# A written TensorE order, 96-row transposes and a shorter feed-forward lag in a fused windowed-attention and feed-forward kernel

## The chip, the cores and the metric

The kernel runs on one core of a Trainium2 chip. The metric is the device time of one execution in microseconds (us). The engines are TensorE (PE; its weight loads are PEld), VectorE (DVE), ScalarE (ACT), GpSimd (POOL) and SyncE (SP), which issues most transfers.

## What is computed

Eight batches with eight heads each hold 512 local and 32 global tokens of head dimension 64. A local token attends to the 32 global tokens and to local tokens at most 32 places away; a global token attends to all 544. The outputs of the heads, side by side, are 4608 rows of 512, and go through a feed-forward network with a squared ReLU:

```python
s_g = scale * q_g @ k_all.T;  out_g = softmax(s_g) @ v_all
s_ll = where(abs(i - j) <= 32, scale * q_l @ k_l.T, -1e9)
out_l = softmax(concat([scale * q_l @ k_g.T, s_ll])) @ v_all
x = concat([out_g, out_l]) as 4608 x 512
out = (s * relu(x @ w_in)**2 + b) @ w_out        # 512 -> 2048 -> 512, float32
```

## The kernel before

Most matmul operands are split in two parts of a shorter float32 format (`F32R`): a rounded high part and the remainder. A product of two split operands is then a sum of several matmuls. ACT casts the high part, and DVE or POOL subtracts.

The work is a loop over steps `j`. A step carries one head through a pipeline. There are 128 heads of 256 queries: eight heads of one half of the sequence and then eight of the other make a batch of 16 steps, and eight heads of a half make one tile of 256 tokens. The first 16 heads (`NF`) go in pairs through an unsplit float32 path while the feed-forward weights are loaded and split (`weight_piece`). From head 16 on, a step issues these TensorE groups, which the text calls by a letter:

- **S** and **G** (`scores`, lines 351 and 357): four matmuls of 192 or 224 columns for the local scores of head `j`, and one of 256 or 288 columns with a 64-column weight for the global tokens' scores. DVE masks and finds the maximum (212), ACT takes the exponential (218), DVE scales (227). The global scores are copied by ACT (361) and added by DVE (362) into `sg`.
- **T** (`p_transposes`, line 306): four float32 transposes of the probabilities of head `j - 1`, 128 by 128 each, split by ACT (367) and DVE (368).
- **P** (`pv_products`, line 378): four matmuls of 128, 192 or 256 columns of head `j - 2`, summed by ACT (389) and DVE (390, 392) into the tile of tokens `x`, which has one buffer.
- **F** (`ffn_in`, line 500): 24 matmuls of 256 columns for one eighth of a tile, feed-forward step `m = j - LAG`, then ACT (506, 514) and DVE (507, 515) for ReLU, square and split.
- **A** (`ffn_out`, line 532): 12 matmuls of 512 columns of feed-forward step `m - 1`, in two accumulators of six each.

Eight feed-forward steps make a tile. After the eighth, `x_split` (472 and 473) makes the split tokens of the next tile `xs`, which has one buffer, in two halves of a cast and a subtraction. Twice in a batch the global tokens of four heads have their softmax (`g_softmax`, at the steps `G_AT`), five transposes (`g_transposes`, three steps later), loads and splits of their values (`g_load`) and products of ten matmuls each, **O** (`g_pv`, line 452). Their outputs go to DRAM, and the last tile, number 16, reads them back (`xg_split`).

PSUM has eight banks: one each for S, G (also used by O), T, P and the two accumulators of A, and two for F. All engines' instruction orders are made by the planner of the tile framework. It simulates the engines, takes what is ready, and prefers what stands earlier in the program; within TensorE too it is free to mix the groups of several steps. The order is then fixed in the program, and each engine runs it in sequence.

The steps end as follows in the loop, and `LAG` is 12:

```python
ffn_in(m)                     # then x_split or xg_split when m % 8 == 7
transposes_and_pv(j - 1, j - 2)
vsp(j - 1)
for fn in extra.pop(j, []): fn()
ffn_out(m - 1)
```

Of the kernel before, what the change touches and what calls it, by code (L numbers as in the profile page):

```python
# [10 lines left out]
F32 = mybir.dt.float32  # L11
F32R = mybir.dt.float32r
# [7 lines left out]
B, H, SL, SG, D = 8, 8, 512, 32, 64  # L20
DM, DF = 512, 2048
P = 128
# [8 lines left out]
NC = 416  # L31
# [12 lines left out]

NF = 16
AHEAD = 0
LAG = 12
WARM_FIRST = 28

SPOTS = (["a","b","c","c","xs"]+["c","c","a","b"]*1+["a","b","c","c"]*12)[:32]  # L50
PIECES = [2, 2, 2, 2, 2, 2, 2, 2, 2, 2, 3, 3, 3, 3]
ACT_DMA = 2
X_ACT = lambda i: i >= 4
G_AT = (13, 18)
G_TR = 3
G_LD = (0, 2)
G_PV = (1, 3)
# [4 lines left out]
def f32(ap):  # L62
    return ap.bitcast(F32)
# [3 lines left out]
def window_attention_then_ffn(ctx: ExitStack, tc: tile.TileContext, qd, qp, qg, kw, vw, vg, w_in, w_out, sv, bv, out):  # L67
# [219 lines left out]
    def chunks(j):  # L287
        b, hf, h = slot(j)
        o = 0
        for blk in range(2):  # L290
            for c in range(2):
                c0, q0, n = CHUNKS[hf, blk][c]
                yield blk, c, c0, q0, n, slice(o, o + n)
                o += n
# [4 lines left out]
    def p_transposes(j):  # L299
        sm = st_.pop(("p", j))  # L300
        p_t = ps.tile([P, 512], F32, tag="t", name=f"ps_t{j}")
        first = 64 if slot(j)[1] == 0 else 0
        st_["pst", j] = p_t[:, first:first + NC]
        for blk, c, c0, q0, n, o in chunks(j):
            at = first + o.start - q0
            nc.tensor.transpose(out=p_t[:, at:at + P], in_=sm[:, c0:c0 + P], identity=ident)  # L306
            if c == 1:
                yield

    def transposes32(i):  # L310
        pt = st_["ptp", i] = sb.tile([P, 2, NC], F32, tag="pt", name=f"ptp{i}")
# [32 lines left out]
    def scores(j):  # L344
        b, hf, h = slot(j)
        ks, qs = st_.pop(("ks", j)), st_.pop(("qs", j))
        p_s = ps.tile([P, 512], F32, tag="s", name=f"ps_s{j}")
        for blk in range(2):
            cols = COLS[hf, blk]
            for a in range(2):  # L350
                nc.tensor.matmul(  # L351
                    p_s[:, cols], lhsT=qs[:, a, blk * P:(blk + 1) * P], rhs=ks[:, cols], start=(a == 0), stop=(a == 1),
                )
        p_g = ps.tile([P, 512], F32, tag="g", name=f"ps_g{j}")
        qgh = st_["qgs", b][:, h]
        ng = 256 + 32 * hf
        nc.tensor.matmul(p_g[0:64, 0:ng], lhsT=qgh, rhs=own(ks, hf), start=True, stop=True)
        softmax([j], [p_s])

        tg = sb.tile([P, 288], F32, tag="tg", name=f"tg{j}", bufs=1)  # L360
        nc.scalar.copy(out=tg[0:32, 0:ng], in_=p_g[32:64, 0:ng])
        nc.vector.tensor_add(out=sg_rows(j, 32)[:, hf * 256:hf * 256 + ng], in0=p_g[0:32, 0:ng], in1=tg[0:32, 0:ng])  # L362
# [11 lines left out]
    def pv_products(j):  # L374
        pt, vs = st_.pop(("pt", j)), st_.pop(("vs", j))
        p_o = st_["pso", j] = ps.tile([P, 2, 2, P], F32, tag="o", name=f"ps_o{j}")
        for blk, c, c0, q0, n, o in sorted(chunks(j), key=lambda x: (x[0], -x[1])):
            nc.tensor.matmul(  # L378
                p_o[:, blk, :, q0:q0 + n], lhsT=vs[:, 2 * blk + c], rhs=pt[:, :, o], start=(c == 1), stop=(c == 0),
            )  # L380
            if c == 0:
                yield

    def pv_sum(j):
        b, hf, h = slot(j)
# [11 lines left out]
    def transposes_and_pv(jt, jp):  # L397
        t = p_transposes(jt) if NF <= jt < NS else iter(())
        p = pv_products(jp) if NF <= jp < NS else iter(())
        for _ in range(2):  # L400
            next(p, None)
            next(t, None)
        list(p), list(t)
        if NF <= jp < NS:
            pv_sum(jp)
        if NF <= jt < NS:
            p_split(jt)
# [10 lines left out]
        nc.vector.reciprocal(gs, gs)  # L418
        nc.vector.tensor_scalar_mul(v, v, gs)

    def g_transposes(b, g, c0, c1):
        sg = st_["sg", b, g]
        if c0 == 0:
            st_["pg", b, g] = sb.tile([P, 5, 4, 2, SG], F32R, tag="pg", name=f"pg{b}_{g}", bufs=1)
        pg = st_["pg", b, g]
        if True:
            p_t = ps.tile([P, 4, P], F32, tag="t", name=f"ps_tg{b}_{g}_{c0}")
            for c in range(c0, c1):
                s0 = min(c * P, SGW - P)
                nc.tensor.transpose(out=p_t[:, c - c0, :], in_=sg[:, s0:s0 + P], identity=ident)  # L430
            v = p_t[:, 0:c1 - c0].rearrange("p c (h q) -> p (c h) q", h=4)
            ph, pl = (pg[:, c0:c1, :, i, :].rearrange("p c h q -> p (c h) q") for i in range(2))
            nc.scalar.copy(out=ph, in_=v)
            nc.vector.tensor_sub(out=pl, in0=v, in1=f32(ph))


    def g_load(b, h):
        rv = sb.tile([P, 10 * D], F32, tag="rvg", name=f"rvg{b}_{h}", bufs=1)
# [37 lines left out]
    def xg_split(t):  # L476
        xs = sb.tile([P, 2, 4, HALF], F32R, tag="xs", name=f"xs{t}", bufs=1)
        for i in range(2):
            xr = sb.tile([P, DM], F32, tag="r", name=f"xgr{i}", bufs=2)
            nc.sync.dma_start(xr, xg_d[i * P:(i + 1) * P, :])  # L480
            p_t = ps.tile([P, 4, P], F32, tag="t", name=f"ps_xg{i}")
            for c in range(4):
                nc.tensor.transpose(out=p_t[:, c, :], in_=xr[:, c * P:(c + 1) * P], identity=ident)
            q = slice(i * P, (i + 1) * P)
            nc.scalar.copy(out=xs[:, 0, :, q], in_=p_t)
            nc.vector.tensor_sub(out=xs[:, 1, :, q], in0=p_t, in1=f32(xs[:, 0, :, q]))
        xs_[t] = xs
# [31 lines left out]

    oacc = {}  # L520

    def ffn_out(m):
        t, pr = m // 8, m % 8
        g = gs_.pop(m)
        if pr == 0:
            oacc[t] = [ps.tile([P, DM], F32, tag=f"acc{i}", name=f"acc{t}_{i}") for i in range(2)]
        for i in range(2):
            n = 0
            for k in range(2):
                f = 2 * pr + k  # L530
                for a, e in ((0, 0), (0, 1), (1, 0)):
                    nc.tensor.matmul(  # L532
                        oacc[t][i], lhsT=g[:, a, k, i * P:(i + 1) * P], rhs=wo[:, e, f, :],
                        start=(pr == 0 and n == 0), stop=(pr == 7 and n == 5),
                    )
                    n += 1
        if pr == 7:
            for i in range(2):
                o = sb.tile([P, DM], F32, tag="r", name=f"o{t}_{i}", bufs=2)
                nc.scalar.copy(out=o, in_=oacc[t][i])  # L540
                if t < 16:
                    b, hf = t // 2, t % 2
                    r0 = b * (SL + SG) + SG + hf * HALF + i * P
                    nc.sync.dma_start(out[r0:r0 + P, :], o)
                else:
                    rows = out.rearrange("(b r) d -> b r d", r=SL + SG)[4 * i:4 * i + 4, 0:SG, :]
                    nc.sync.dma_start(rows, o)
# [2 lines left out]
    nc.sync.dma_start(b_t, bv.partition_broadcast(P))  # L550

    NM = NT * 8
    extra, early, late = defaultdict(list), {}, {}
    for b in range(B):
        for g in range(2):
            s0 = 16 * b + G_AT[g]
            extra[s0].append(lambda b=b, g=g: g_softmax(b, g))
            early[s0 + G_TR] = lambda b=b, g=g: g_transposes(b, g, 0, 4)
            late[s0 + G_TR] = lambda b=b, g=g: g_transposes(b, g, 4, 5)
            for i in range(2):  # L560
                h = 4 * g + 2 * i
                extra[s0 + G_TR + G_LD[i]].append(lambda b=b, h=h: g_load(b, h))
                extra[s0 + G_TR + G_PV[i]].append(lambda b=b, h=h: g_pv(b, h))
# [18 lines left out]
    qg_load(0)  # L582
    ld(0)
    ld(2)
    for j in range(NM + LAG + 2):
        sp(j + 1)
        if j + 4 < NF:
            ld(j + 4)
        if j + 2 >= NF:
            ld(j + 2)  # L590
        vl(j)
        for _ in range(PIECES[j] if j < len(PIECES) else 0):
            weight_piece(piece)
            piece += 1
        if j < NS:
            b1 = j // 16 + 1
            if j % 16 == 14 and b1 < B:
                qg_load(b1)
            sc(j)
            if j % 16 == 15 and NF <= j + 1 < NS:  # L600
                qg_split(b1)
        if j in early:
            early.pop(j)()
        m = j - LAG
        if 0 <= m < NM:
            ffn_in(m)
            if m % 8 == 7:
                t = m // 8 + 1
                if t < 16:
                    x_split(t)  # L610
                elif t == 16:
                    xg_split(16)
        tr(j - 1)
        transposes_and_pv(j - 1, j - 2)
        vsp(j - 1)
        for fn in extra.pop(j, []):
            fn()
        pvs(j - 2)
        if j == 0:
            vl32(0)  # L620
        vl32(j + 2)
        if j == 9:
            x_split(0)
        if 0 <= m - 1 < NM:
            ffn_out(m - 1)
        if j in late:
            late.pop(j)()
    assert piece == 32 and not extra


# [73 lines left out]
```

## Time and profile before

| | |
|---|---|
| time, median of 3 runs | 1049.52 us (1049.19 to 1052.2) |
| time of the profiled execution | 1050.66 us |
| its span, first to last instruction | 1048.0 us |
| mean granted TensorE clock | 0.986 |
| PE busy | 1008.9 us (96%), 7060 matmuls |
| PEld busy | 908.8 us (87%) |
| DVE busy | 816.4 us (78%) |
| ACT busy | 710.1 us (68%) |
| POOL busy | 311.8 us (30%) |

Busy time is the time in which an engine has at least one instruction in work. Matmuls overlap: the recorded duration of one is longer than the distance to the next. The profile is of one execution; the times are of others of the same program.

### The profile page before, as it was taken

How to read it: one execution, taken by the hardware profiler on the slowest of the kernel's cores; microseconds unless marked ns; L12 is line 12 of the kernel's file. 1: busy time of each engine (PE TensorE's matmuls, PEld its weight loads, DVE VectorE, ACT ScalarE, POOL GpSimd, SP SyncE). 2: the span in 40 equal slices, each digit the busy share in tenths (PEclk: the TensorE clock that was granted, in tenths of full speed). 3: DMA queues.
4: the chain of work that ended last, by engine and by line, in shares of the span. 5: the costliest groups of instructions: out<-in, count | busy, mean ns of one | idle time of the engine just before them, and what ended most of it. 6: DMA issues, size and time to landing. Idle time of an engine off the chain costs nothing.

```text
span 1048.0 us, 20280 instructions
## 1 busy us (share of the span) xinstructions
PE 1008.9 (96%) x7060; PEld 908.8 (87%) x7060; DVE 816.4 (78%) x2096; ACT 710.1 (68%) x1816; POOL 311.8 (30%) x365
## 2 busy tenths in 40 slices
PE   6689999999999999999999999999999999999996
PEld 3378999989999899989998899988998899999895
DVE  6999878887798878888798778888699778863321
ACT  6997867777587667777587667777687667743221
POOL 0000634333343324333343324333343324211000
PEclk8789999999999999999999999999999999999998
DMA  8764322312132222312132122312132122101000
GB/s 297 255 218 142 95 65 72 95 47 91 48 114 57 62 66 76 96 47 91 47 111 60 54 74 76 96 48 90 48 109 62 49 80 67 55 2 48 22 21 20
DMA packets 62254, 85.73 MB, mean 82 GB/s; under 512 B 7368, under 2 KB 49352, under 8 KB 62152
## 3 DMA queue, kind: packets, MB, share of 16 engines
q1 hardware_dynamic: 61864, 83.39, 25.8%
q8 instruction: 55, 0.90, 0.4%
q10 hardware_dynamic: 288, 1.05, 0.3%
q14 instruction: 47, 0.39, 0.1%
HBM read 74.97 MB, written 9.44 MB: 81 GB/s over the span
## 4 chain that ended last, share of the span: by engine, by line
PE 62%; DVE 22%; ACT 10%; issue 3%; DMA 2%; DVEq 0%; ACTq 0%; SPq 0%
PE acc L532 26%; PE ps_h L500 25%; DVE sm L227 4%; PE ps_t L306 3%; ACT sm L218 3%; PE ps_s L351 3%; DVE r L507 3%; DVE x L392 2%; PE ps_o L378 2%; DVE pt L368 2%; DVE sm L212 2%; DVE kq L189 2%; DVE sg L362 1%; DVE g L515 1%; DVE u L390 1%
## 5 line engine op out<-in xcount | busy, mean ns | idle before, releaser
L500 PE MATMUL ps_h<-xs,wi 128*128 128x256 f32 x3264 | 441.3, 282 | 4.6 <-DVE r L507 2.1
L500 PEld LDWEIGHTS ps_h<-xs,wi 128*128 128x128 f32 x3264 | 414.5, 188 | 18.4 <-DVE r L507 3.1
L532 PE MATMUL acc<-wo,g 128*128 128x512 f32 x1632 | 427.0, 396 | 0.0
L532 PEld LDWEIGHTS acc<-wo,g 128*128 128x128 f32 x1632 | 288.4, 188 | 49.9 <-ACT wst L146 0.2
L218 ACT ACTIVATE sm<-sm,nm 128x224 f32<-128x224 f32 (+1 forms) x256 | 118.4, 465 | 69.9 <-DVE nm L212 69.0
L199 POOL TENSOR_TENSOR vs<-rv,vs 128x256 fp32r<-128x256 f32 x112 | 95.3, 851 | 234.3 <-ACT vs L198 205.2
L514 ACT ACTIVATE g<-r,b_t 128x512 fp32r<-128x512 f32 x136 | 98.3, 723 | 89.0 <-DVE r L507 88.4
L191 POOL TENSOR_TENSOR kq<-rq,kq 128x256 fp32r<-128x256 f32 x112 | 89.6, 800 | 189.6 <-ACT kq L190 185.2
L515 DVE SCALAR_TENSOR_TENSOR g<-r,b_t,g 128x512 fp32r<-128x512 f32 x136 | 104.3, 767 | 52.2 <-ACT g L514 52.1
L507 DVE SCALAR_TENSOR_TENSOR r<-ps_h,s_t,r 128x512 f32<-128x512 f32 x136 | 101.4, 746 | 52.5 <-ACT r L506 51.9
L506 ACT ACTIVATE r<-ps_h 128x512 f32<-128x512 f32 x136 | 81.0, 596 | 57.9 <-PE ps_h L500 56.1
L306 PE MATMUL ps_t<-ident,sm 128*128 128x128 f32 x512 | 96.3, 282 | 10.4 <-ACT sm L225 6.9
L189 POOL TENSOR_TENSOR kq<-rk,kq 64x416 fp32r<-64x416 f32 x56 | 62.0, 1108 | 123.3 <-ACT kq L188 121.8
L227 DVE TENSOR_SCALAR sm<-sm,ss 128x192 f32<-128x192 f32 (+1 forms) x224 | 91.9, 452 | 3.2
L378 PE MATMUL ps_o<-pt,vs 128*128 128x256 f32 x448 | 84.4, 283 | 0.0
L212 DVE CUSTOM_DVE_ANT_0 sm<-ps_s,mask 128x192 f32<-128x192 f32 (+1 forms) x224 | 75.2, 364 | 10.1 <-PE ps_s L351 9.4
L351 PE MATMUL ps_s<-kq 128*128 128x192 f32 (+1 forms) x448 | 79.8, 277 | 0.0
L444 POOL TENSOR_TENSOR vsg<-rvg,vsg 128x320 fp32r<-128x320 f32 x64 | 58.5, 934 | 69.8 <-ACT vsg L443 69.7
L392 DVE TENSOR_TENSOR x<-u 64x256 f32<-64x256 f32 x112 | 75.4, 673 | 3.6
L306 PEld LDWEIGHTS ps_t<-ident,sm 128*128 128x128 f32 x512 | 58.0, 144 | 16.6 <-ACT ptp L314 5.7
L351 PEld LDWEIGHTS ps_s<-kq 128*128 128x128 f32 x448 | 67.2, 190 | 5.0 <-DVE nm L212 0.2
L378 PEld LDWEIGHTS ps_o<-pt,vs 128*128 128x128 f32 x448 | 67.7, 190 | 2.8
(83 smaller groups left out, 1182.2 us busy)
## 6 DMA issues: line engine op xcount, KB each, us to landing
rq<-in_qd SPq DMA_DIRECT2D x112, 128.0 KB, 2.3
rv<-in_vw SPq DMA_DIRECT2D x112, 128.0 KB, 2.1
rk<-in_kw SPq DMA_DIRECT2D x56, 208.0 KB, 2.4
rvg<-in_vg SPq DMA_DIRECT2D x32, 320.0 KB, 2.9
out<-o SPq DMA_DIRECT2D x34, 256.0 KB, 2.5
wst<-in_w_in SPq DMA_DIRECT2D x15, 512.0 KB, 4.8
wst<-in_w_out SPq DMA_DIRECT2D x15, 512.0 KB, 4.2
rvp<-in_vw SPq DMA_DIRECT2D x8, 256.0 KB, 3.7
```

The lines of the kernel that those rows point to most:

```text
L212: nc.vector.tensor_tensor_reduce(out=sm[:, c], in0=p_s[:, c], in1=mask, op0=ALU.add, op1=ALU.min, scale=-scale, scalar=BIG, accum_out=nm[: ...
L218: nc.scalar.activation(out=p, in_=p, func=AF.Exp, bias=nm[:, n:n + 1], scale=-1.0, accum_out=ss[:, n:n + 1],)
L227: nc.vector.tensor_scalar(out=p, in0=p, scalar1=ss[:, n:n + 1], scalar2=1.0, op0=ALU.mult, op1=ALU.mult,)
L306: nc.tensor.transpose(out=p_t[:, at:at + P], in_=sm[:, c0:c0 + P], identity=ident)
L351: nc.tensor.matmul(p_s[:, cols], lhsT=qs[:, a, blk * P:(blk + 1) * P], rhs=ks[:, cols], start=(a == 0), stop=(a == 1),)
L378: nc.tensor.matmul(p_o[:, blk, :, q0:q0 + n], lhsT=vs[:, 2 * blk + c], rhs=pt[:, :, o], start=(c == 1), stop=(c == 0),)
L392: nc.vector.tensor_add(out=x[q0:q0 + 64, h // 2, :].rearrange("p (k q) -> p k q", k=2), in0=u[0:64], in1=u[64:128],)
L500: nc.tensor.matmul(p_h[:, k], lhsT=wi[:, a, c, f * P:(f + 1) * P], rhs=xs[:, e, c, :], start=(n == 0), stop=(n == 11),)
L507: nc.vector.scalar_tensor_tensor(out=r, in0=p_h, scalar=s_t, in1=r, op0=ALU.mult, op1=ALU.mult)
L514: nc.scalar.activation(out=g[:, 0], in_=r, func=AF.Identity, bias=b_t)
L515: nc.vector.scalar_tensor_tensor(out=g[:, 1], in0=r, scalar=b_t, in1=f32(g[:, 0]), op0=ALU.add, op1=ALU.subtract,)
L532: nc.tensor.matmul(oacc[t][i], lhsT=g[:, a, k, i * P:(i + 1) * P], rhs=wo[:, e, f, :], start=(pr == 0 and n == 0), stop=(pr == 7 and n == 5),)
```

## The change

From step 20 on, TensorE's instructions are pinned to program order; the other engines stay with the planner. Within a step the program order becomes: scores, transposes mixed with products, F, global work, A. Of the scores, the matmul G moves between the two matmuls of the 192-column block. The four T of a head are sorted so that the two narrow chunks come first, and a narrow chunk whose queries start at row 0 of its block is transposed with 96 rows and a 96-column identity in place of 128. P and T are taken in the order P P T T T P P T. The feed-forward runs ten steps behind in place of twelve. The global softmaxes move from steps 13 and 18 to 12 and 16 of a batch, and all that hangs on them moves along; the global transposes are issued in two parts, one ahead of each accumulator of A, the single one in G's bank, and their copies have high priority. The last tile's two halves use two PSUM banks (T's and S's) and a staging buffer of P's operands. The split tokens keep one buffer, as before.

```diff
-LAG = 12
+LAG = 10
+ORDERED = 20
-G_AT = (13, 18)
+G_AT = (12, 16)
@@ p_transposes
-        for blk, c, c0, q0, n, o in chunks(j):
+        for blk, c, c0, q0, n, o in sorted(chunks(j), key=lambda x: x[1]):
             at = first + o.start - q0
-            nc.tensor.transpose(out=p_t[:, at:at + P], in_=sm[:, c0:c0 + P], identity=ident)
-            if c == 1:
-                yield
+            q = 96 if c == 0 and q0 == 0 else P
+            nc.tensor.transpose(out=p_t[:, at:at + q], in_=sm[0:q, c0:c0 + P], identity=ident[0:q, 0:q])
+            yield
@@ scores
                 nc.tensor.matmul(
                     p_s[:, cols], lhsT=qs[:, a, blk * P:(blk + 1) * P], rhs=ks[:, cols], start=(a == 0), stop=(a == 1),
                 )
-        nc.tensor.matmul(p_g[0:64, 0:ng], lhsT=qgh, rhs=own(ks, hf), start=True, stop=True)
+                if blk == hf and a == 0:
+                    nc.tensor.matmul(p_g[0:64, 0:ng], lhsT=qgh, rhs=own(ks, hf), start=True, stop=True)
@@ transposes_and_pv
-        for _ in range(2):
-            next(p, None)
-            next(t, None)
+        for which in (p, p, t, t, t, p, p, t):
+            next(which, None)
@@ g_transposes
+        for c0, c1, tag in ((4, 5, "g"), (0, 4, "t")):
...
+            with tc.high_priority():
+                nc.scalar.copy(out=ph, in_=v)
+                nc.vector.tensor_sub(out=pl, in0=v, in1=f32(ph))
+            yield
@@ xg_split
-            xr = sb.tile([P, DM], F32, tag="r", name=f"xgr{i}", bufs=2)
+            xr = sb.tile([P, 2 * NC], F32, tag="pt", name=f"xgr{i}")[:, 0:DM]
-            p_t = ps.tile([P, 4, P], F32, tag="t", name=f"ps_xg{i}")
+            p_t = ps.tile([P, 4, P], F32, tag="ts"[i], name=f"ps_xg{i}")
@@ ffn_out(m, turn)
         for i in range(2):
+            next(turn, None)
@@ the loop over steps
+    fixed = ExitStack()
     for j in range(NM + LAG + 2):
+        if j == ORDERED:
+            fixed.enter_context(tc.manual_schedule(engines={mybir.EngineType.PE}))
...
+        tr(j - 1)
+        transposes_and_pv(j - 1, j - 2)
+        vsp(j - 1)
+        pvs(j - 2)
...
         m = j - LAG
+        if m == -1:
+            x_split(0)
         if 0 <= m < NM:
             ffn_in(m)
...
         for fn in extra.pop(j, []):
             fn()
         if 0 <= m - 1 < NM:
-            ffn_out(m - 1)
+            ffn_out(m - 1, turns.pop(j, iter(())))
+        else:
+            list(turns.pop(j, ()))
+    fixed.close()
```

## Rows read from the trace of the kernel before

**Rows 1.** Busy time by stretch: us, PE, PEld, DVE, ACT, POOL, clock, DMA, GB/s.

```profile
60.00:100.00 40.00, 38.16 (x285) 33.13 (x286) 38.92 (x86) 34.30 (x79) 1.01 (x1) 1.00 0.60 196
```

**Rows 2.** Busy time by stretch, one batch of sixteen steps, same columns.

```profile
448.43:566.62 118.19, 116.96 (x834) 107.58 (x835) 98.09 (x259) 84.20 (x221) 42.73 (x50) 1.00 0.24 73
```

**Rows 3.** Timeline of PE at a batch border; idle time before in brackets.

```profile
566.62 0.35 PE L357 MATMUL ps_g<-kq,qgs 128*64 128x288 f32 x1 [0.60 <-DVE sg L362]
```

**Rows 4.** Waits of PE, 200 to 900 us: total, times, longest.

```profile
PE ps_g L357 <- DVE sg L362: 4.2, 7, 0.7
PE ps_h L500 <- DVE r L507: 2.1, 6, 0.4
PE ps_h L500 <- DVE xs L473: 1.6, 6, 0.3
```

**Rows 5.** Timeline of PE, 500 to 508 us: start, duration, instructions merged.

```profile
502.17 0.60 PE L306 MATMUL ps_t<-ident,sm 128*128 128x128 f32 x4
...
502.94 2.29 PE L500 MATMUL ps_h<-xs,wi 128*128 128x256 f32 x18
505.06 2.90 PE L532 MATMUL acc<-wo,g 128*128 128x512 f32 x12
507.81 0.28 PE L500 MATMUL ps_h<-xs,wi 128*128 128x256 f32 x1
```

**Rows 6.** Timeline of all engines, 524 to 537 us, matmuls and weight loads.

```profile
527.22 0.38 PE L306 MATMUL ps_t<-ident,sm 128*128 128x128 f32 x2
...
527.36 0.38 PE L357 MATMUL ps_g<-kq,qgs 128*64 128x288 f32 x1
...
527.58 1.32 PE L532 MATMUL acc<-wo,g 128*128 128x512 f32 x5
...
532.57 0.77 PE L452 MATMUL ps_og<-vsg,pg 128*64 128x128 f32 x10
...
533.30 0.53 PEld L351 LDWEIGHTS ps_s<-kq 128*128 128x128 f32 x4
```

**Rows 7.** Groups by line and form: busy, mean ns, idle before.

```profile
L351 PEld LDWEIGHTS ps_s<-kq 128*128 128x128 f32 x448 | 67.2, 190 | 5.0 <-DVE nm L212 0.2
...
L306 PEld LDWEIGHTS ps_t<-ident,sm 128*128 128x128 f32 x512 | 58.0, 144 | 16.6 <-ACT ptp L314 5.7 <-issue 5.2 <-ACT sm L225 3.8
...
L452 PE MATMUL ps_og<-vsg,pg 128*64 128x128 f32 x320 | 25.5, 224 | 0.0
```

**Rows 8.** Timeline of all engines, 524 to 537 us, around one token split.

```profile
524.15 2.38 PE L500 MATMUL ps_h<-xs,wi 128*128 128x256 f32 x19
...
526.61 0.60 ACT L506 ACTIVATE r<-ps_h 128x512 f32<-128x512 f32 x1
...
526.93 0.46 PE L378 MATMUL ps_o<-pt,vs 128*128 128x256 f32 x2
527.11 0.61 ACT L472 CAST xs<-x 128x512 fp32r<-128x512 f32 x1
...
529.02 0.68 DVE L473 TENSOR_TENSOR xs<-x,xs 128x512 fp32r<-128x512 f32 x1
...
530.57 0.62 DVE L392 TENSOR_TENSOR x<-u 64x256 f32<-64x256 f32 x1
...
531.22 0.62 ACT L472 CAST xs<-x 128x512 fp32r<-128x512 f32 x1 [0.48 <-DVE x L392]
...
532.17 0.74 DVE L515 SCALAR_TENSOR_TENSOR g<-r,b_t,g 128x512 fp32r<-128x512 f32 x1
...
532.84 0.67 DVE L473 TENSOR_TENSOR xs<-x,xs 128x512 fp32r<-128x512 f32 x1
```

**Rows 9.** Waits of SP's queue, 200 to 900 us.

```profile
SPq L461 <- DVE xr L460: 66.5, 18, 5.0
```

**Rows 10.** Timeline of PE at the last tile, 985 to 1048 us.

```profile
993.18 0.50 PE L500 MATMUL ps_h<-xs,wi 128*128 128x256 f32 x2 [0.68 <-ACT xs L485]
...
993.90 7.74 PE L500 MATMUL ps_h<-xs,wi 128*128 128x256 f32 x64 [0.22 <-DVE xs L486]
```

More of the change, by code (lines that the diff above doesn't have):

```diff
@@ L347, in scores @@
         p_s = ps.tile([P, 512], F32, tag="s", name=f"ps_s{j}")
+        p_g = ps.tile([P, 512], F32, tag="g", name=f"ps_g{j}")
+        qgh = st_["qgs", b][:, h]
+        ng = 256 + 32 * hf
         for blk in range(2):
@@ L353, in scores @@
                 )
-        p_g = ps.tile([P, 512], F32, tag="g", name=f"ps_g{j}")
-        qgh = st_["qgs", b][:, h]
-        ng = 256 + 32 * hf
-        nc.tensor.matmul(p_g[0:64, 0:ng], lhsT=qgh, rhs=own(ks, hf), start=True, stop=True)
+                if blk == hf and a == 0:
+                    nc.tensor.matmul(p_g[0:64, 0:ng], lhsT=qgh, rhs=own(ks, hf), start=True, stop=True)
         softmax([j], [p_s])
@@ L380, in pv_products @@
             )
-            if c == 0:
-                yield
+            yield
     def pv_sum(j):
@@ L419, in g_softmax, with g_transposes @@
         nc.vector.tensor_scalar_mul(v, v, gs)
-    def g_transposes(b, g, c0, c1):
+    def g_transposes(b, g):
         sg = st_["sg", b, g]
[L423 to L427, printed above, removed]
+        pg = st_["pg", b, g] = sb.tile([P, 5, 4, 2, SG], F32R, tag="pg", name=f"pg{b}_{g}", bufs=1)
+        for c0, c1, tag in ((4, 5, "g"), (0, 4, "t")):
+            p_t = ps.tile([P, 4, P], F32, tag=tag, name=f"ps_tg{b}_{g}_{c0}")
             for c in range(c0, c1):
@@ L432, in g_transposes @@
             ph, pl = (pg[:, c0:c1, :, i, :].rearrange("p c h q -> p (c h) q") for i in range(2))
-            nc.scalar.copy(out=ph, in_=v)
-            nc.vector.tensor_sub(out=pl, in0=v, in1=f32(ph))
+            with tc.high_priority():
+                nc.scalar.copy(out=ph, in_=v)
+                nc.vector.tensor_sub(out=pl, in0=v, in1=f32(ph))
+            yield
     def g_load(b, h):
@@ L520, in window_attention_then_ffn, with ffn_out @@
     oacc = {}
-    def ffn_out(m):
+    def ffn_out(m, turn):
         t, pr = m // 8, m % 8
@@ L552, in window_attention_then_ffn @@
     NM = NT * 8
-    extra, early, late = defaultdict(list), {}, {}
+    extra, turns = defaultdict(list), {}
     for b in range(B):
@@ L557, in window_attention_then_ffn @@
             extra[s0].append(lambda b=b, g=g: g_softmax(b, g))
-            early[s0 + G_TR] = lambda b=b, g=g: g_transposes(b, g, 0, 4)
-            late[s0 + G_TR] = lambda b=b, g=g: g_transposes(b, g, 4, 5)
+            turns[s0 + G_TR] = g_transposes(b, g)
             for i in range(2):
@@ L601, in window_attention_then_ffn @@
                 qg_split(b1)
-        if j in early:
-            early.pop(j)()
+        tr(j - 1)
+        transposes_and_pv(j - 1, j - 2)
+        vsp(j - 1)
+        pvs(j - 2)
+        if j == 0:
+            vl32(0)
+        vl32(j + 2)
         m = j - LAG
+        if m == -1:
+            x_split(0)
         if 0 <= m < NM:
@@ L612, in window_attention_then_ffn @@
                     xg_split(16)
-        tr(j - 1)
-        transposes_and_pv(j - 1, j - 2)
-        vsp(j - 1)
         for fn in extra.pop(j, []):
             fn()
[L618 to L623, printed above, removed]
         if 0 <= m - 1 < NM:
-            ffn_out(m - 1)
-        if j in late:
-            late.pop(j)()
+            ffn_out(m - 1, turns.pop(j, iter(())))
+        else:
+            list(turns.pop(j, ()))
+    fixed.close()
     assert piece == 32 and not extra
```

## Prediction

> **What bounds the kernel now.** I read the busy time by stretches first. From 60 us on TensorE works almost without a pause: 38.16 of 40 us, at a granted clock of 1.00, the 2.4 GHz level [rows 1]. Sixteen steps (one batch) in the middle take 118.19 us: PE 116.96, DVE 98.09, ACT 84.20 [rows 2]; it is one of five in a row that take 118.2 to 118.3. Their border is one wait that returns, the last time shown at 566.62 us [rows 3]. Then the waits: between 200 and 900 us PE stands for 4.2 us before G, 2.1 and 1.6 us before F [rows 4], 7.9 in 700, or 1.3 us in sixteen steps. So PE sets the pace, and waits are 1% of it.
>
> A busy PE need not be at its best rate, so the third view is the timeline, for the spacing of matmuls [rows 5]: eighteen F take 502.94 to 505.06, 0.118 us each; twelve A until 507.81, 0.229 each; four T last 0.60, and two 0.38 [rows 6], so (0.60 - 0.38) / 2 = 0.11 apart. Ten O (128 columns, 64-column weights) last 0.77, (0.77 - 0.22) / 9 = 0.061 apart [rows 6, 7]. Columns thus cost 0.46 ns each (0.118 / 256), except in T. Four S weight loads last 0.53, (0.53 - 0.19) / 3 = 0.113 apart [rows 6, 7], though S streams 192 or 224 columns, worth 0.09 or 0.10. I conclude: a matmul costs the longer of its own columns and the next one's weight load, some 0.112 us for 128 weight columns, 0.06 for 64. This is an inference from rows; the sum rests on it.
>
> **The change, part by part.**
>
> *Written order.* From step 20 each step is S and G, then P and T mixed, then 24 F, then 12 A. By the rule above, one head of the first half: S 0.090 (G's 64-column load is next), G 0.118, S 3 x 0.112, together 0.54; P 0.118, P 0.08 (a T's load, between 0.061 and 0.11, follows its 0.061), T 0.11, T of 96 rows 0.082 (below), T 0.112, P 0.118, P 0.090, T 0.112, together 0.82. The second half's head has two 96-row T and comes to 0.56 + 0.79. The mean is 1.36. Sixteen steps: heads 16 x 1.36 = 21.7; F and A 16 x (24 x 0.118 + 12 x 0.229) = 89.3; global work 40 O x 0.061 and 10 transposes x 0.11, some 3.7 with their borders. Sum 114.7 against 118.19: 3.5 us less, if PE never waits. Of that, 1.3 is today's waits, some 0.7 the 96 rows, and the rest, 1.5, I put to short matmuls that stand before a full weight load today and to the load that follows each wait. Steps 20 to 127 are 108, or 6.75 such stretches: 23.6 us at most.
>
> *96-row transposes.* Three of eight per pair of halves lose 32 columns and 32 rows: 1.5 x 108 = 162 of them. If T's cost is its columns, each saves 0.11 x 32 / 128 = 0.027, together 4.4 us (within the 23.6); the other bound is nothing. A row decides between them: the second T of a pair starts at 527.33, the G behind it, with only a 64-column load, at 527.36, and the next A at 527.58 [rows 6]. That is 0.25 from T to A; G's 288 columns are 0.133 of it, so T holds PE for 0.11 though the load behind it is short. I take 0.027. The Trainium skill, page "TensorE: Matmul & The Clock Gate", section "LDWEIGHTS (loading the stationary operand)", speaks against it: a weight load's time goes by its columns, whatever the rows. The 96-row T still loads 128 columns. By that page alone a T between T would be bound by its load and save nothing; the T loads here are recorded at 144 ns against 190 for S [rows 7], so this trace does not show one price for both.
>
> *Ten heads behind, and one buffer of split tokens.* The tile of tokens has one buffer, its split another. The split of tile t can start when the last F of tile t-1 has ended and must be there when the first F of tile t comes. In the written order 12 A (2.75) and the next head (1.36) lie between, 4.1 us, and six F more (0.7) before the second half is read: 4.8. Today the split takes: F ends at 526.53, first cast 527.11, its subtraction 529.02, second cast 531.22, and that subtraction ends 533.51, 7.0 us after the F [rows 8]. If it stays 7.0, PE waits 2.2 us per tile. But the second cast waited for the last head's tokens (L392 until 531.19, 3.8 us after its P ended at 527.39). In the written order that P lies before the 24 F (2.83 us), so its tokens come about 1.0 us after the F's end; the first cast would end at 1.2, the second at 1.8 to 2.4, its subtraction, after the DVE queue of 1.0 to 1.3 that both halves show, at 3.5 to 4.4. That fits into 4.8 with less than one DVE instruction to spare. I book 0.3 us a tile, bounds 0 and 2.2: 14 tiles, 4 us. Behind a waiting F stand all other F, A and the next head's S, and softmax and ReLU wait for those; today PE takes A, S or P meanwhile, later it cannot.
>
> *Other single buffers.* Scores, transposes, P, G and O have one PSUM bank each, drained while 36 F and A run (5.6 us). The shortest cover is that of the four global transposes: six A, S and P, 2.1 us, against a cast and a subtraction of 512 columns, 0.61 + 0.68 by the split's rows. The longest chain is ReLU, square and split: from F's end at 526.53 to 532.91, 6.4 us [rows 8], with 7.1 to go until its A. I book 0.03 us a step: 3 us; bounds 0 and 0.3.
>
> *Global softmax earlier.* It goes one step earlier for one half of the heads, two for the other, with its transposes, value loads (two transfers on SP's queue, two casts on ACT, two subtractions on POOL each) and O with their stores. Costs PE nothing; it frees the global score rows before the next batch's first G writes them, and today's waits before G [rows 3, 4] are for that addition. SP stands up to 5.0 us at a store [rows 9]; loads behind it are issued two steps, 14 us, ahead. POOL is busy 42.73 of 118.19 [rows 2]. I take 0. Without that cover a late load would hold S by what it is late.
>
> *Start and end.* F is put two steps earlier in the free part; between 60 and 100 us it could fill at most 1.8 us of idle PE [rows 1], and its two ACT and two DVE instructions a step could delay the float32 heads as much: 0, bounds -2 and +2. At the last tile PE now waits 0.68 and 0.22 us for its split [rows 10]; with both transposes in banks of their own and 12 A as cover that goes: -0.9.
>
> **Sum.** 23.6 + 0.9 - 4 - 3 = 17.5 us less than the profiled execution's 1050.66: 1033. The median of the runs is 1.1 below that execution, so 1032.
>
> **The rivals.**
>
> *The 96 rows save nothing* (each T bound by its own load): 162 x 0.027 = 4.4 back, 1036. The pair at 527.33 speaks against it. The page named above would have it so.
>
> *DVE's queue shows.* DVE is busy 98.09 of 118.19 us; in 114.7 it would be 86%. The chain F to A takes 6.4 of 7.1 us. Where DVE falls behind, a PE in fixed order waits, and free filling is gone. At 0.18 us a step 19 us go, 16 more than booked: 1048; from 0.19 on nothing is won. For it: a DVE that is nearly full in bursts. Against: the waits of 1% today under the same load.
>
> *The split of the tokens holds PE* (the other side): if it takes 7.0 us and more as now, 14 x 2.2 = 31 us instead of the 4 booked, so 1032 + 27 = 1059. It decides at a split of about 6.3 us (21.5 / 14 = 1.5 beyond 4.8) from F's end to the second subtraction's end; below that the kernel is faster. For it: the row of 7.0 us and one buffer. Against: 2.3 us or so of those are the late tokens, which the order brings forward.
>
> **How the numbers follow.** About 3 us, 0.3%, is what a measurement of this kernel can tell from no change. Chances: forecast 0.47 (1025 to 1037); 96 rows for nothing 0.15 (1031 to 1041); DVE's queue 0.20 (1040 to 1053, half of it within 3 us of now); split of tokens 0.18 (1053 and more). Faster: 0.47 + 0.15 + 0.11 = 0.73; the same 0.09; slower 0.18. The range for 8 in 10 leaves out the lowest 0.05 and the worst 0.15: 1022 to 1055.
>
> **What the profile after would show.** Right: sixteen steps in 115 to 116 us, F always in runs of 24 and A in runs of 6 or 12, no wait before G, pairs of 96-row T at 0.08, waits before F of tile starts under 0.5 us. Wrong: waits of 1 us and more before F by L473, or before A or T by DVE in every step; 96-row T still 0.11 apart; or the first 130 us longer than now.

## The result, and the profile after

The changed kernel takes 1035.81 us in the median of six runs (1033.59 to 1037.46), beside 1050.01 for the kernel before, also of six: a ratio of 0.9861, with an interval of 0.9851 to 0.9871. Forecast were 1032 and a range of 1022 to 1055. One execution of a later kernel, e6 below, took 1970 us beside 1033 to 1034 in its four others; its ratio leaves it out, and its cause is open. The profiled execution took 1035.21 us with a span of 1033.4. In the profile after, F is line 499, T 308, P 380, S 355, G 359, O 451, and the global transposes are line 428.

Busy time of two batches of sixteen steps, columns as in [rows 2]:

```profile
370.94:486.10 115.16, 114.65 (x835) 106.35 (x835) 97.17 (x259) 84.02 (x222) 41.28 (x49) 1.00 0.26 75
486.10:601.29 115.19, 114.68 (x834) 106.34 (x835) 97.17 (x259) 84.09 (x221) 41.28 (x49) 1.00 0.25 75
```

A batch takes 115.2 us in place of 118.19 [rows 2]. TensorE's waits between 200 and 900 us, answering to [rows 4]:

```profile
PE ps_t L308 <- DVE pg L433: 3.0, 6, 0.5
```

The three waits of before are gone. One new one has come, six times 0.5 us, once in a batch. The timeline of PE shows a whole step, and that wait in the step after it:

```profile
589.59 2.96 PE L532 MATMUL acc<-wo,g 128*128 128x512 f32 x12
592.38 0.25 PE L355 MATMUL ps_s<-kq 128*128 128x192 f32 x1
592.47 0.28 PE L359 MATMUL ps_g<-kq,qgs 128*64 128x256 f32 x1
592.59 0.49 PE L355 MATMUL ps_s<-kq 128*128 128x192 f32 x3
592.92 0.35 PE L380 MATMUL ps_o<-pt,vs 128*128 128x256 f32 x2
593.11 0.48 PE L308 MATMUL ps_t<-ident,sm 128*128 128x128 f32 x3
593.34 0.45 PE L380 MATMUL ps_o<-pt,vs 128*128 128x256 f32 x2
593.63 0.27 PE L308 MATMUL ps_t<-ident,sm 128*128 128x128 f32 x1
593.66 3.05 PE L499 MATMUL ps_h<-xs,wi 128*128 128x256 f32 x24
596.55 0.27 PE L428 MATMUL ps_tg<-ident,sg 128*128 128x128 f32 x1
596.58 1.62 PE L532 MATMUL acc<-wo,g 128*128 128x512 f32 x6
598.04 0.63 PE L428 MATMUL ps_tg<-ident,sg 128*128 128x128 f32 x4
598.43 1.64 PE L532 MATMUL acc<-wo,g 128*128 128x512 f32 x6
...
601.29 0.52 PE L308 MATMUL ps_t<-ident,sm 128*128 128x128 f32 x3 [0.51 <-DVE pg L433]
```

The written order is seen at once: S with G inside, P P T T T P P T, 24 F without a break, A in two sixes with the global transposes ahead of each. The last row is the wait: T needs its bank, which still holds the four global transposes of 598.04 until DVE has subtracted them.

The split of the tokens at a tile border, answering to [rows 8] (the F before ends at 525.68):

```profile
524.82 0.86 PE L499 MATMUL ps_h<-xs,wi 128*128 128x256 f32 x6
...
526.21 1.14 ACT L471 CAST xs<-x 128x512 fp32r<-128x512 f32 x2
...
527.44 1.28 DVE L472 TENSOR_TENSOR xs<-x,xs 128x512 fp32r<-128x512 f32 x2
...
529.53 0.71 PE L499 MATMUL ps_h<-xs,wi 128*128 128x256 f32 x4
```

Both halves are there at 528.72, 3.0 us after the last F, and the next tile's F starts at 529.53 behind P and T, not behind the split. Before, the split took 7.0 us.

The last tile, answering to [rows 10]: eight transposes, twelve A as cover, and F without a wait.

```profile
973.46 1.04 PE L482 MATMUL ps_xg<-ident,xgr 128*128 128x128 f32 x8
...
974.25 3.00 PE L532 MATMUL acc<-wo,g 128*128 128x512 f32 x12
...
977.09 2.96 PE L499 MATMUL ps_h<-xs,wi 128*128 128x256 f32 x24
```

The place where time was lost is the border between the planner's order and the written one, on PE's timeline at step 20:

```profile
133.07 0.60 PE L428 MATMUL ps_tg<-ident,sg 128*128 128x128 f32 x4
133.46 0.33 PE L359 MATMUL ps_g<-kq,qgs 128*64 128x256 f32 x1
136.24 0.48 PE L428 MATMUL ps_tg<-ident,sg 128*128 128x128 f32 x1 [2.44 <-DVE sg L364]
137.39 0.47 PE L359 MATMUL ps_g<-kq,qgs 128*64 128x256 f32 x1 [0.68 <-DVE pg L433]
...
139.68 4.43 PE L499 MATMUL ps_h<-xs,wi 128*128 128x256 f32 x24
```

and the busy time and granted clock around it (clock is the third number from the right):

```profile
134.00:136.00 2.00, 0.00 (x0) 0.00 (x0) 1.97 (x3) 1.57 (x4) 0.92 (x2) 0.97 0.14 41
136.00:138.00 2.00, 1.08 (x4) 0.79 (x5) 1.10 (x3) 0.36 (x2) 0.40 (x1) 0.50 0.66 198
...
142.00:144.00 2.00, 2.00 (x16) 2.00 (x16) 1.16 (x5) 0.00 (x0) 0.01 (x1) 0.82 0.51 167
144.00:146.00 2.00, 2.00 (x18) 1.74 (x17) 1.19 (x3) 1.83 (x5) 0.43 (x1) 1.00 0.00 1
```

Step 19's single global transpose and step 20's G use G's bank one after the other. PE stands 2.44 and 0.68 us. The granted clock falls to 0.50, the 1.2 GHz level, while PE still stands for the first time: its mean is 0.97 from 134 to 136 us, where no matmul runs, and 0.50 in the next 2 us. The 24 F take 4.43 us in place of 3.05.

Where the 14.6 us of span came from can be counted by F's matmuls, 24 to a step. The same three parts of the work, before and after (busy times and counts of F alone; the first column is the stretch and its length):

```profile
0.00:220.10 220.10, 71.81 (x528) 67.43 (x529) 15.63 (x21) 13.13 (x22) 0.95 0.46 150
220.10:922.10 702.00, 310.74 (x2280) 290.53 (x2281) 71.56 (x96) 56.52 (x95) 1.00 0.24 71
922.10:1048.00 125.90, 58.71 (x456) 56.59 (x455) 14.24 (x19) 11.35 (x19) 0.97 0.07 23
```

```profile
0.00:226.00 226.00, 72.46 (x529) 67.38 (x529) 16.36 (x22) 13.16 (x22) 0.92 0.46 147
226.00:909.70 683.70, 290.29 (x2280) 274.04 (x2281) 70.58 (x95) 56.80 (x95) 1.00 0.24 73
909.70:1033.40 123.70, 56.56 (x456) 55.70 (x456) 14.25 (x19) 11.36 (x19) 0.97 0.07 24
```

The first 22 feed-forward steps (22 x 24 = 528 matmuls; the counts miss that by one at the edge of a stretch) end 5.9 us later than before, the next 95 take 18.3 us less, and the rest 2.2 less: 5.9 - 18.3 - 2.2 = -14.6.

### The profile page after: what moved, and what is told of

Its sections match the earlier page's. It is cut to its first block, busy times and chain, and to the rows that moved or that the text cites. A ratio compares the mean times of both kernels' runs of the same rounds, so it can differ in the third digit from the quotient of the medians.

```text
span 1033.4 us, 20334 instructions
## 1 busy us (share of the span) xinstructions
PE 998.6 (97%) x7060; PEld 904.7 (88%) x7060; DVE 813.8 (79%) x2096; ACT 710.4 (69%) x1816; POOL 300.2 (29%) x365
## 4 chain that ended last, share of the span: by engine, by line
PE 85%; ACT 5%; DVE 5%; DMA 3%; issue 1%; SPq 0%; DVEq 0%; ACTq 0%
PE ps_h L499 34%; PE acc L532 34%; PE ps_t L308 5%; PE ps_o L380 4%; PE ps_s L355 4%; PE ps_og L451 2%; DMA wst<-in_w_out 2%; PE ps_g L359 1%; ACT sm L219 1%; ACT wst L147 1%; DVE g L514 1%; DVE x L393 1%; DMA b_t<-in_bv 1%; DVE r L506 1%; ACT g L513 1%
## 5 line engine op out<-in xcount | busy, mean ns | idle before, releaser
L499 PE MATMUL ps_h<-xs,wi 128*128 128x256 f32 x3264 | 419.3, 284 | 0.0
L532 PE MATMUL acc<-wo,g 128*128 128x512 f32 x1632 | 405.0, 395 | 0.5 <-ACT g L513 0.5
L499 PEld LDWEIGHTS ps_h<-xs,wi 128*128 128x128 f32 x3264 | 397.1, 190 | 3.3 <-issue 0.5
L514 DVE SCALAR_TENSOR_TENSOR g<-r,b_t,g 128x512 fp32r<-128x512 f32 x136 | 120.3, 885 | 57.6 <-ACT g L513 57.0
L308 PE MATMUL ps_t<-ident,sm 128*128 128x128 f32 (+1 forms) x512 | 96.8, 277 | 7.9 <-DVE pg L433 3.0
L363 ACT COPY tg<-ps_g 32x256 f32<-32x256 f32 (+1 forms) x112 | 42.3, 378 | 72.3 <-PE ps_g L359 71.7
L380 PE MATMUL ps_o<-pt,vs 128*128 128x256 f32 x448 | 91.0, 285 | 0.0
L391 DVE TENSOR_TENSOR u<-ps_o,u 128x256 f32<-128x256 f32 x112 | 47.3, 422 | 41.8 <-ACT u L390 40.0
L308 PEld LDWEIGHTS ps_t<-ident,sm 128*128 128x128 f32 (+1 forms) x512 | 58.4, 145 | 13.3 <-ACT ptp L315 4.6
L228 DVE TENSOR_SCALAR sm<-sm,ss 128x192 f32<-128x192 f32 (+1 forms) x224 | 68.0, 346 | 1.0
```

What stands on the lines that cost most here:

```text
L308: nc.tensor.transpose(out=p_t[:, at:at + q], in_=sm[0:q, c0:c0 + P], identity=ident[0:q, 0:q])
L380: nc.tensor.matmul(p_o[:, blk, :, q0:q0 + n], lhsT=vs[:, 2 * blk + c], rhs=pt[:, :, o], start=(c == 1), stop=(c == 0),)
L499: nc.tensor.matmul(p_h[:, k], lhsT=wi[:, a, c, f * P:(f + 1) * P], rhs=xs[:, e, c, :], start=(n == 0), stop=(n == 11),)
L514: nc.vector.scalar_tensor_tensor(out=g[:, 1], in0=r, scalar=b_t, in1=f32(g[:, 0]), op0=ALU.add, op1=ALU.subtract,)
L532: nc.tensor.matmul(oacc[t][i], lhsT=g[:, a, k, i * P:(i + 1) * P], rhs=wo[:, e, f, :], start=(pr == 0 and n == 0), stop=(pr == 7 and n == 5),)
```

## The experiments

All times are medians. "Sixteen steps" is the time from the start of feed-forward step 38 to that of step 102, divided by four; the last column adds up PE's waits between 200 and 900 us. Ratios are to the kernel before, run beside each.

| kernel | time, us | ratio (interval) | sixteen steps, us | PE waits, us |
|---|---|---|---|---|
| before | 1050 | 1 | 118.22 | 7.9 |
| changed | 1035.8 | 0.9861 (0.9851 to 0.9871) | 115.19 | 3.0 |
| e1: order from 18 | 1034.5 | 0.9849 (0.9830 to 0.9868) | 115.23 | 3.0 |
| e2: 128-row T | 1040.4 | 0.9899 (0.9883 to 0.9915) | 115.18 | none |
| e3: planner's order | 1035.6 | 0.9855 (0.9834 to 0.9875) | 115.18 | 1.1 |
| e4: P and T alternate | 1038.8 | 0.9887 (0.9870 to 0.9905) | 115.59 | none |
| e5: global T in S's bank | 1040.3 | 0.9893 (0.9874 to 0.9911) | 115.85 | 4.6 |
| e6: order from 24 | 1034.2 | 0.9832 (0.9816 to 0.9847) | 115.18 | 3.1 |
| e7: planner, old global steps | 1083.0 | 1.0301 (1.0282 to 1.0320) | 123.12 | 22.5 |
| e8: planner, lag 12 | 1031.4 | 0.9811 (0.9792 to 0.9830) | 115.23 | 1.2 |
| e9: before, global steps alone | 1042.1 | 0.9920 (0.9893 to 0.9948) | 115.82 | 0.2 |
| e10: e8 with 128-row T | 1036.7 | 0.9868 (0.9847 to 0.9890) | 116.31 | 0.6 |
| e11: order from 24, lag 12 | 1096.2 | 1.0443 (1.0426 to 1.0461) | 122.88 | 30.1 |
| e12: e9 with 96-row T | 1038.1 | 0.9888 (0.9871 to 0.9905) | 115.58 | none |

**e1, the border two steps earlier.** The theory was that the loss at the border belongs to step 19's transposes; the rival, that any border costs it.

```diff
-ORDERED = 20
+ORDERED = 18
```

> Only the first ordered step moves, from 20 to 18. Theory (seam): the changed kernel loses about 5 us once, at 133.8 to 144 us, because step 19's single global transpose and G share one bank across the border between free and written order: two PE waits of 2.4 and 0.7 us and then matmuls at half the granted clock. With the border two steps ahead of these transposes the two waits go, and the time is 1030 to 1032. Rival (any border costs this, wherever it lies): waits of 3 us and a lower clock appear at the new border and the time stays at 1035 to 1037.

The time is 1034.5, the same as the changed kernel's within the noise (the intervals of the two ratios overlap). The waits moved with the border: 1.9 us before G for the global output's copy (L456) at 121.6 us and 0.9 us before the next G for the addition to the global scores. The theory in its narrow form fell; e6 asks again.

**e2, all transposes with 128 rows.**

```diff
-            q = 96 if c == 0 and q0 == 0 else P
+            q = P
```

> All transposes take 128 rows and columns again. Theory (a transpose costs its columns): 1.5 x 108 transposes in written order go back from 0.084 to 0.11 us, and the time rises by 4 us, to 1039 to 1041. Rival (a transpose is bound by its weight load): no change, 1035 to 1036.5.

The time rose by 4.6 us, as the theory said, but not in the way it said: sixteen steps take 115.18 us as before. First the rows. Three T of a second-half head (96, 96 and 128 rows) last 0.44 us in the changed kernel:

```profile
542.89 0.44 PE L308 MATMUL ps_t<-ident,sm 96*128 96x96 f32 x3
```

and with 128 rows throughout, in e2:

```profile
545.11 0.49 PE L308 MATMUL ps_t<-ident,sm 128*128 128x128 f32 x3
```

That is 0.05 less for two distances, 0.025 for each 96-row T: its cost follows its columns, though it loads 128 columns of weights. In the written order the batch does not get shorter by these 24 x 0.025 = 0.6 us, because the new wait of 0.5 us before T takes their place; with 128 rows no wait is listed. The loss lies at the ends. The profiled executions differ by 3.0 us of span: 2.5 of them come before feed-forward step 22, 0.6 behind step 117, and none between. In e2's profile the waits at the border are 4.1 us in place of 3.1, and one before T of 0.75 near 919 us in place of 0.13; what makes the rest of the loss at the start is open.

**e3, no written order.** Everything else of the change stays, and the planner orders TensorE throughout.

```diff
-ORDERED = 20
+ORDERED = -1
```

> The whole change without the written order: the planner orders TensorE throughout. Theory (the order itself gives the pairing of short matmuls, 1.5 us in sixteen steps, and takes the waits away): sixteen steps take 117 to 118 us, and the time is 1043 to 1047. Rival (the waits went because of the earlier global softmax and the shorter lag, the order adds nothing): sixteen steps take under 116 us, and without a border the time is 1030 to 1034.

The theory fell. Without the written order a batch takes the same 115.2 us, PE waits 1.1 us in 700, and the time is the same. The rival was half right: the time stayed at 1035.6 rather than falling to 1034 or less. So the other edits give the gain of a steady batch without the order. What the order would give without them is open: no run has it with the global softmaxes at steps 13 and 18.

**e4, P and T in strict alternation.**

```diff
-        for which in (p, p, t, t, t, p, p, t):
+        for which in (p, t, p, t, p, t, p, t):
```

> P and T strictly alternate (P T P T P T P T) in place of P P T T T P P T. Theory (a matmul costs the longer of its own columns and the next one's weight load): the 96-row transposes now stand before a full load and two more T do, 0.033 us more in a head of the first half and 0.06 in one of the second, 5 us in 108 steps: 1040 to 1042, and sixteen steps 115.9 us. Rival (weight loads are hidden, only columns count): no change, 1035 to 1036.5.

Sixteen steps take 115.59 us with no wait listed. The changed kernel without its 0.5 us wait would take 115.19 - 0.51 = 114.68, so the pairing is worth 0.9 us in sixteen steps; the rule gives 16 x 0.047 = 0.75. That fits columns against the next weight load, and not the rival. The time, 1038.8, is below the 1040 to 1042 that were expected, because the changed kernel's wait is gone here; probably the longer work ahead of T covers it, as in e2.

**e5, another bank for the four global transposes.** This was to take the remaining wait away.

```diff
-        for c0, c1, tag in ((4, 5, "g"), (0, 4, "t")):
+        for c0, c1, tag in ((0, 4, "s"), (4, 5, "g")):
```

> The written order stays; the four global transposes go first and into the scores' bank, the single one second into G's. Theory (the one wait of 0.5 us in sixteen steps, T before the global copies, is the price of a bank with too short a cover): the wait goes, sixteen steps take 114.6 to 114.7 us, and the time falls by some 3.5 us to 1032 to 1033. Rival (another copy is late in its place): a wait of 0.4 us or more in sixteen steps at S or G, and the time stays at 1035 to 1037.

The rival holds. The wait moved to G, which stands 0.78 us until the single transpose's copies are done, behind those of the four:

```profile
600.40 0.60 PE L428 MATMUL ps_tg<-ident,sg 128*128 128x128 f32 x4
...
602.21 0.27 PE L428 MATMUL ps_tg<-ident,sg 128*128 128x128 f32 x1
...
604.73 0.33 PE L359 MATMUL ps_g<-kq,qgs 128*64 128x256 f32 x1 [0.78 <-DVE pg L433]
```

**e6, the border at step 24**, where no global transpose is near.

```diff
-ORDERED = 20
+ORDERED = 24
```

> The first ordered step is 24. Theory (the loss at the border comes from global products and transposes that the planner left behind in the free part and that hold G's bank; after step 22 there are none until step 28): no wait of over 0.3 us within 10 us of the border, and the time is 1030 to 1032. Rival (every border costs 3 us and a clock drop): again 1034 to 1037.

The time is 1034.2, and the interval of the ratio lies just below the changed kernel's: by the medians 1.6 us less, by the ratios 3. The theory fell: the border still costs 0.90 and 1.11 us, with O of an earlier step and two G behind each other in one bank:

```profile
164.38 0.76 PE L451 MATMUL ps_og<-vsg,pg 128*64 128x128 f32 x10
166.05 0.33 PE L359 MATMUL ps_g<-kq,qgs 128*64 128x256 f32 x1 [0.90 <-DVE og L456]
167.48 0.35 PE L359 MATMUL ps_g<-kq,qgs 128*64 128x288 f32 x1 [1.11 <-DVE sg L364]
...
168.52 3.08 PE L499 MATMUL ps_h<-xs,wi 128*128 128x256 f32 x24
```

Two standing times of about 1 us here did not lower the clock: the granted clock stays at 1.00 from 160 to 176 us, and 24 F take 3.08 us. The borders at 18, 20 and 24 so cost 2.8, 3.1 and 2.0 us of waits, all around G's bank. The first two also lost the clock: in e1 the granted clock is 0.50 from 126 to 128 us, 0.84 and 0.81 in the 2 us before and behind. So every border tried costs, and the size depends on what stands there. That the planner leaves G and O of the last free steps late is what the rows suggest; no run changed that alone.

**e7, the planner's order with the old global steps.** Both parts of the global transposes use T's bank here, so two things differ from e3.

```diff
-ORDERED = 20
+ORDERED = -1
-G_AT = (12, 16)
+G_AT = (13, 18)
-        for c0, c1, tag in ((4, 5, "g"), (0, 4, "t")):
+        for c0, c1, tag in ((0, 4, "t"), (4, 5, "t")):
```

> The planner orders TensorE throughout, and the global softmaxes are at steps 13 and 18 again, with all five transposes in T's bank, as before the change. Theory (the earlier global softmax took the waits of G for the addition to the global scores away): 0.6 us of wait before G return in sixteen steps, which take 115.8 to 116.4 us; the time is 1040 to 1043. Rival (the shorter lag did it all): sixteen steps stay at 115.2 us and the time at 1034 to 1037.

The direction is the theory's, the size is not: 123.1 us in sixteen steps, with P waiting for the split of T's bank, ten times and 16.1 us in 700:

```profile
551.29 0.48 PE L380 MATMUL ps_o<-pt,vs 128*128 128x256 f32 x2 [1.84 <-DVE pt L370]
```

So this run mixes the late steps with the shared bank, and e9 was made to part them.

**e8, the planner's order with the lag of before.**

```diff
-ORDERED = 20
+ORDERED = -1
-LAG = 10
+LAG = 12
```

> The planner orders TensorE throughout, and the feed-forward runs twelve steps behind again. Theory (the shorter lag took the two waits of F at the tile borders away, since the split of tokens no longer holds up the next tile's first heads): waits of 0.3 us before F return twice in sixteen steps, which take 116 to 117 us; the time is 1041 to 1047. Rival (the lag is of no account for a planner that mixes steps anyway): sixteen steps stay at 115.2 us and the time at 1034 to 1037.

The theory fell, and the rival was half right: sixteen steps stay at 115.2 us, but the time falls to 1031.4, below the kernel before, the changed kernel and e3, with intervals that don't touch. It is the fastest kernel here. The lag of ten brings a free TensorE nothing; the lag of twelve is 4.2 us better than e3 by the medians. Of the 3.0 us between the two profiled executions, 1.1 come before feed-forward step 22, 2.0 behind step 117, and none between. How the lag makes them is open.

**e9, one edit to the kernel before.**

```diff
-G_AT = (13, 18)
+G_AT = (12, 16)
```

> The kernel before with one edit: the global softmaxes at steps 12 and 16. Theory (the waits of before hang on the global scores' buffer, which the next batch needs while the late global softmax still reads it): the wait of 0.6 us before G goes and those of F get smaller, sixteen steps take 116.2 to 117.4 us in place of 118.2, and the time is 1038 to 1045. Rival (the gain of the planner's order comes from the other edits): sixteen steps stay at 118 us and the time at 1049 to 1052.

Sixteen steps take 115.82 us, better than expected. The row is the time of 64 feed-forward steps, 463.28 / 4 (F alone is counted):

```profile
369.47:832.75 463.28, 207.41 (x1536) 191.19 (x1536) 47.71 (x64) 38.24 (x64) 1.00 0.25 74
```

This edit alone gives 2.4 of the 3.0 us that a batch gained. The time falls by 8 us only. In its profile the first 22 feed-forward steps end 3.4 us later than before, with waits of 2.2 and 0.8 us at 181 to 187 us, and the next sixteen still take 118.65 us; the two waits at the last tile stay.

**e10, 128-row transposes in e8.**

```diff
-            q = 96 if c == 0 and q0 == 0 else P
+            q = P
```

> The planner orders TensorE throughout, the lag is twelve, and all transposes take 128 rows. Beside the same kernel with 96 rows (1031.4 us, 115.2 us in sixteen steps). Theory (24 transposes in sixteen steps cost 0.025 us more each, and no wait absorbs it): sixteen steps take 115.8 to 115.9 us, and the time is 1035 to 1036. Rival (as in the written order, where 128 rows left the sixteen steps at 115.2): no change, 1030 to 1032.

Sixteen steps take 116.31 us, 1.08 more than in e8, where the transposes' own 24 x 0.025 explain 0.6. That is more than the theory's 115.9, and the time, 1036.7, just above its 1036. The rest may lie in the planner's order, which is another one; no run shows that.

**e11, lag 12 in the written order.**

```diff
-LAG = 10
-ORDERED = 20
+LAG = 12
+ORDERED = 24
```

> Written order from step 24, with the feed-forward twelve steps behind. Theory (in a written order ten is what the one buffer of the tile of tokens asks for: at twelve, two heads of the next tile are summed before the split has read the old tile, and what follows stands behind them): PE waits of 1 us and more at each tile border, sixteen steps of 117 to 120 us, and 1045 to 1065. Rival (the lag matters only for the start, as in the planner's order, where twelve was 4 us faster than ten): sixteen steps of 115.2 us and 1029 to 1032.

The theory holds, and more strongly than expected: P waits 3.5 and 2.1 us in turn at the tile borders, and a batch takes 122.9 us. One border on all engines:

```profile
439.82 1.29 DVE L472 TENSOR_TENSOR xs<-x,xs 128x512 fp32r<-128x512 f32 x2
...
442.12 1.31 DVE L393 TENSOR_TENSOR x<-u 64x256 f32<-64x256 f32 x1
...
443.46 0.37 ACT L390 COPY u<-ps_o 128x256 f32<-128x256 f32 x1 [0.60 <-DVE x L393]
...
444.54 0.71 PE L380 MATMUL ps_o<-pt,vs 128*128 128x256 f32 x2 [3.49 <-DVE ss L222]
```

The split (472) ends at 441.11; only then can the sum of the next tile's first head (393) enter the one token buffer; the copy for the next head's sum (390) waits for it, and P, whose bank 390 and DVE's sum behind it (391, until 444.39) read, for those. The row of P names 222, the next instruction in DVE's queue.

**e12, two edits to the kernel before.**

```diff
-G_AT = (13, 18)
+G_AT = (12, 16)
-            nc.tensor.transpose(out=p_t[:, at:at + P], in_=sm[:, c0:c0 + P], identity=ident)
+            q = 96 if c == 0 and q0 == 0 else P
+            nc.tensor.transpose(out=p_t[:, at:at + q], in_=sm[0:q, c0:c0 + P], identity=ident[0:q, 0:q])
```

> The kernel before with two edits: the global softmaxes at steps 12 and 16, and the 96-row transposes. Theory (these two carry the whole gain of a steady batch; order, lag, pairing and banks add nothing to it): sixteen steps take 115.0 to 115.3 us, as in the changed kernel, and the time is 3.5 to 7 us under that with the first edit alone (1042.1 us): 1035 to 1038.5. Rival (the two do not add up, since the planner finds other work late): sixteen steps stay at 115.7 us or more, and the time at 1040 to 1043.

The time is in the expected stretch, 1038.1; sixteen steps take 115.58 us, between theory and rival. The two edits carry 2.6 of the 3.0 us.

## Why the prediction was right, and where its steps failed

The direction, the size within 4 us and the range held. That the size came so close is in part luck: the steady part gained more than was booked, the start lost what nobody had booked, and the two nearly cancel. By its steps:

*Written order, the sum of a batch.* Forecast 114.7 us if PE never waits; measured 115.19 with one wait of 0.51, so 114.68. The rule behind it, own columns against the next weight load, fits e4. But the cause was put in the wrong place. The step credits the order with 3.5 us; the same edits without the order reach 115.18 (e3). What the order adds by pairing, about 0.5 us over e3, its own new wait takes back.

*Global softmax earlier.* This is the step that failed: "Costs PE nothing ... I take 0". The edit alone takes a batch from 118.22 to 115.82 (e9). The step named the buffer of the global scores, which the next batch needs, and then booked the waits of before, 1.3 us, under the order. It also took the wait before G at the batch border [rows 3] for the one that this buffer makes. The rows say otherwise. That wait is of the batch's last head; the addition it stands for is that of the head before, which ran at 566.12 us, 2.1 us after its copy had ended, behind other work of DVE and with no global transpose near. The buffer holds at the next batch's first head, where no wait of PE is listed. In the kernel before, that head's addition comes 13.1 us after its copy, behind the single global transpose, which still reads the scores of the old batch:

```profile
575.26 0.36 ACT L361 COPY tg<-ps_g 32x256 f32<-32x256 f32 x1
...
586.19 0.27 PE L430 MATMUL ps_tg<-ident,sg 128*128 128x128 f32 x1
...
588.74 0.40 DVE L362 TENSOR_TENSOR sg<-ps_g,tg 32x256 f32<-32x256 f32 x1
```

and in e9, at the same border, 8.7 us after it:

```profile
562.91 0.36 ACT L361 COPY tg<-ps_g 32x256 f32<-32x256 f32 x1
...
571.93 0.41 DVE L362 TENSOR_TENSOR sg<-ps_g,tg 32x256 f32<-32x256 f32 x1 [0.28 <-PE ps_tg L430]
```

Until the addition G's bank is taken. In the kernel before the next G starts 0.06 us behind it, in each of the five batches looked at; in e9 8.9 us behind it, so there the bank no longer holds G. At the fifth head of a batch the distance from copy to addition falls from 11.6 to 3.9 us. In the changed kernel and in e3 it is 1.0 us or less at both heads. This fits the buffer as the cause, through a planner that has to put other work in between, but the edit moves softmax, transposes, loads and O together, and no run moves one of them alone. The gain is also larger than the listed waits: the other 1.1 us may be worse pairs of matmuls in the order of before, but no run shows that.

*96 rows.* 0.027 forecast, 0.025 measured. The rival by which they save nothing fell for the matmul itself: the 96-row T is 0.025 cheaper with the same 128 weight columns. Against it the prediction cites the Trainium skill, page "TensorE: Matmul & The Clock Gate", section "LDWEIGHTS (loading the stationary operand)": the time of a load goes by its columns, whatever its rows. The recorded loads of T in the changed kernel agree, 144 ns on average with 96 rows and 145 with 128. What fell is that the load sets the distance from one T to the next. A batch gains nothing by the edit in the written order (e2), 0.24 us in one order of the planner (e9 to e12) and 1.08 in another (e8 to e10).

*Ten heads behind, split of tokens.* Booked 4 us, measured 0: the split is there after 3.0 us, and the next tile's F comes after 3.85, where 4.1 were reckoned (4.8 for its second half). The reason stated, that the tokens of the last head come before the F and not after, is seen in the rows, and both halves follow each other without a gap. The rival of 1059 us did not come. e11 shows the same buffer from the other side: two heads more, and it costs 7.7 us a batch.

*Other single buffers.* Booked 3 us over the whole, measured 3.0 between 200 and 900 us, all in the place that the step named as the shortest cover. The rival of DVE's queue did not come: no other wait is listed there.

*Start and end.* The end gained what was forecast, and more: no wait at the last tile, and 2.2 us less behind step 117. The start was taken as 0 with bounds of 2 us, and it is the term that was mis-sized: the first 22 feed-forward steps end 5.9 us later. Of this the border's waits are 3.1 and the 24 F at the lower clock 1.4 us; S, P and T at that clock add to it. The prediction didn't think of the border as a place at all. It named a longer start as a sign of being wrong, but in the first 130 us, and there both kernels have started 240 F; the loss comes just behind. Without the border (e3) the 22 steps end 3.9 us earlier than in the changed kernel, and the time is the same by the medians.

The sum then reads, in the spans of the profiled executions: 18.3 less in 95 feed-forward steps, 2.2 less at the end, 5.9 more at the start, 14.6 less together (15.4 by their times); forecast were 17.5. Over its 108 steps the prediction booked 23.6 - 4 - 3 = 16.6 less, where 6.75 x 3.03 = 20.5 were there to gain; the start took back most of the difference.

## What to carry to other kernels

When a free planner and a written order end at the same time per batch, look for what both had in common: here the steps of the global softmaxes, one line of the change, which brings the readers of a single buffer forward. A buffer can be held without any listed wait of the engine that sets the pace, as here for 13 us a batch: it shows in the distance between a copy and the addition behind it. A sum of work per step tells what a kernel can reach, not which edit gets it there, so each edit wants a run by itself. And a written order makes every single buffer's cover exact: it has to be counted step by step, at the place where the order begins as well, and a lag that is free elsewhere may then cost 6%.

## What was not expected of the hardware

TensorE's granted clock fell to 0.50 within 2.44 us of standing still, and was back at 1.00 by 144 us; it fell in e1 too, there only behind 1.94 us, one matmul and 0.90; two waits of 0.90 and 1.11 us in e6, 0.3 us of work apart, left it at 1.00. A float32 transpose of 128 columns holds TensorE for 0.11 us, where 128 columns of a split operand take 0.06, and it gets cheaper with its columns.
